# Two score computations placed between the second and third weight of an FFN step

## The chip, the cores and the metric

The kernel runs on one core of one Trainium2 chip. The metric is the device time of one execution in microseconds (us). A core has five engines that run their own instruction streams and meet only at semaphores: TensorE (PE, matrix products, with its weight loads shown as PEld), VectorE (DVE), ScalarE (ACT), GpSimd (POOL) and SyncE (SP). The last two mostly start transfers (DMAs) here. Products are written to PSUM, which has eight banks of 128 x 512 fp32; all other on-chip data are in SBUF.

## The reference

The computation is a low-rank attention (eight batches, eight heads, 1024 positions, head size 64; keys and values are projected from 1024 positions to 64), followed by a feed-forward network that takes the maximum of three products:

```python
k_proj = np.einsum('ks,bhsd->bhkd', E, k)
v_proj = np.einsum('ks,bhsd->bhkd', F, v)
scores = scale * np.matmul(q, k_proj.transpose(0, 1, 3, 2))
scores = scores - np.max(scores, axis=-1, keepdims=True)
attn = np.exp(scores)
attn = attn / (np.sum(attn, axis=-1, keepdims=True) + 1e-09)
attn_out = np.matmul(attn, v_proj)
x = attn_out.transpose(0, 2, 1, 3).reshape(8192, 512)
h = np.maximum(np.maximum(x @ w1, x @ w2), x @ w3)      # 512 -> 768
out = h @ w_out                                         # 768 -> 512
```

## The kernel before

The kernel goes through the eight batches. The feed-forward part of a batch is done in two halves (`ch` 0 and 1) of 512 positions. A half has six steps of `up` (`jt` 0 to 5, one for each 128 of the 768 hidden columns) and then four of `down` (128 positions each). In a step of `up`, PE makes twelve matmuls of 128 x 128 by 128 x 512: four for each of w1, w2 and w3, each weight into one PSUM bank. ScalarE copies the first bank to SBUF (`h1s`), VectorE takes the maximum of the copy and the second bank (`m12`) and then that of `m12` and the third bank (`hT`). `down` multiplies `hT` by w_out, ScalarE copies the result to `o_sb`, and SP's queue writes it out.

The attention of batch b+1 is laid between these steps while batch b's feed-forward part runs. `plan(b)` is a table from (half, step) to a list of pieces of attention; `behind(ch, step)` issues the pieces of an entry after that step. The pieces are:

- `qd`: VectorE repacks q, and SP's queue starts transposing transfers (line 331) that write q transposed into `qT`. For batch 1 there are two of them, one for each half of the head pairs, issued after step 7 of batch 0's first half.
- `kproj`, `kt`: the key projection (16 matmuls, L284), its transpose (L351) and a VectorE copy into `kpT`.
- `sc(b, g)`: scores of head pair g. Four small matmuls (L200, from `qT` and `kpT`) fill two banks. The exponential that reads them (`pT`, L211, ScalarE) isn't issued at once: it is put on the list `later`, which `run_later` works off in the next `up`, right after that step's `h1s` copy, or in the next `down` after its copy.
- `vproj`: the value projection (16 matmuls, L284) and four copies into `vp`, two on ScalarE and two on VectorE.
- `ld`: three loads for a batch further on, issued on POOL's queue.
- `za(b, g)`: the sums of the exponentials and the products with the values (L220, four matmuls each, two banks each), then on ScalarE the logarithm of the sums (`zl`, L233) and the exponential of its negative, the inverse (`zi`, L239), and on VectorE the product of the two (`xT`, L250), which frees the banks of the values.

The order of each engine's instructions is the order in which this code issues them. The PSUM banks are dealt by a small model of the engines' times inside the kernel (`clock`, `free`, `bank`, `two`): a new piece gets the bank, or the pair of banks, that the model expects to be free first. The semaphore waits follow from the data and from the banks dealt.

For the work around the change, batch 0's second half, the order before is: step 0, `kproj(1)`, step 1, `kt(1)`, step 2, then `sc(1,0)`, `sc(1,1)`, `vproj(1)`, `ld(2)`, step 3, `za(1,0)`, `sc(1,2)`, step 4, `za(1,1)`, `sc(1,3)`, step 5, `za(1,2)`, and the four `down` steps, with `za(1,3)` after the second of them.

Of the kernel before, what the change touches and what calls it, by code (L numbers as in the profile page):

```python
# [15 lines left out]
def kernel(  # L16
# [62 lines left out]
    def bank():  # L79
        n = min(range(8), key=lambda n: free[n])  # L80
        deal((n,))
        return psum_t[:, n, :], (n,)
# [5 lines left out]
    def runs(eng, ready, dt, ns=()):  # L88
        if eng in clock:
            clock[eng] = max(clock[eng], ready + 0.06) + dt  # L90
            for n in ns:
                free[n] = clock[eng]
            return clock[eng]
        return ready + dt
# [3 lines left out]
    def copy(eng, o, i, ns=(), dt=0.65):  # L98
        done = {  # L99
            "v": nc.vector.tensor_copy, "s": nc.scalar.copy, "g": nc.gpsimd.tensor_copy  # L100
        }[eng](out=o, in_=i)
        runs(eng, clock["pe"] if ns else 0.0, dt, ns)
        return done
# [89 lines left out]
    def scores(b, g, lo, nsi):  # L193
        t, ns = two()
        n = nsi // 2
        for c in range(2):
            for hp in range(2):
                rows = slice(hp * HALF, (hp + 1) * HALF)
                at = g * SI + lo + c * n
                nc.tensor.matmul(  # L200
                    out=t[c * HALF:(c + 1) * HALF, hp, 0:n * P],
                    lhsT=kpTs[b][rows, g, :],
                    rhs=qTs[b][rows, at:at + n, :],
                    start=True, stop=True,
                )
        return t[:, :, 0:n * P], ns, pe(n * MM / 4 + 0.1)

    def exps(b, g, lo, nsi, sc):
        t, ns, ready = sc
        pTs[b, g, lo] = att.tile([P, 2, CHUNK], BF16, name="pT", bufs=4)[:, :, 0:nsi * HALF]  # L210
        nc.scalar.activation(out=pTs[b, g, lo], in_=t, func=AF.Exp, scale=scale)  # L211
        runs("s", ready, 0.17 + nsi * 0.107, ns)
# [45 lines left out]
    def run_later():  # L258
        for f in later:
            f()  # L260
        later.clear()

    def sc(b, g, lo=0, nsi=SI):
        def f():
            t = scores(b, g, lo, nsi)
            later.append(lambda: exps(b, g, lo, nsi, t))
        return f
# [12 lines left out]
    def proj(b, kv, t, heads, width):  # L280

        for si in range(SI):
            for hh in range(2):
                nc.tensor.matmul(  # L284
                    out=t[hh * HALF:(hh + 1) * HALF, 0:width],
                    lhsT=efT[:, si, (kv - 1) * KP:kv * KP],
                    rhs=qkv[b][kv][:, heads[hh], si, :],
                    start=(si == 0), stop=(si == SI - 1),
                )
        pe(8 * (width * 0.00042 + 0.01))  # L290
# [72 lines left out]
    def vproj(b):  # L363
        def f():
            t, ns = bank()
            proj(b, 2, t, (LO, HI), 4 * D)

            vps[b] = att.tile([P, H, D], BF16, name="vp")
            for hh, hs in enumerate((LO, HI)):
                i = t[hh * HALF:(hh + 1) * HALF, 0:4 * D].rearrange("a (h d) -> a h d", d=D)  # L370
                for to in range(2):
                    copy("sv"[hh], vps[b][to * HALF:(to + 1) * HALF, hs, :], i, ns, 0.4)
        return f
# [120 lines left out]
    def up_mm(h, i, b, ch, jt, cts, first=0, last=NCT - 1):  # L494
        for ct in cts:
            nc.tensor.matmul(  # L496
                out=h,
                lhsT=w_sb[i][:, ct, jt * P:(jt + 1) * P],
                rhs=xTs[b][:, ct, ch * SPC:(ch + 1) * SPC, :],
                start=(ct == first),  # L500
                stop=(ct == last),
            )
            pe(MM)

    def most(o, h, ns, other, ready=0.0):
        nc.vector.tensor_tensor(out=o, in0=h, in1=other, op=ALU.max)  # L506
        return runs("v", max(clock["pe"], ready), 0.69, ns)
# [27 lines left out]
                most(hs[:, jt] if i == 1 else hTs[0, 0][:, jt, :], *h[jt], hs[:, jt])  # L535
                then((i, jt))

    def up(b, ch, jt):
        if jt == 0:
            hTs[b, ch] = ffn_sb.tile([P, NJT, CHUNK], BF16, name="hT")  # L540
        h, done = [], []
        early = jt == 0
        for i in range(3):
            h.append(bank())
            up_mm(h[i][0], i, b, ch, jt, range(NCT - early))
            done.append(clock["pe"])
        if early:
            for i in range(3):
                up_mm(h[i][0], i, b, ch, jt, (NCT - 1,))
                done[i] = clock["pe"]  # L550
        h1s = ffn_sb.tile([P, CHUNK], FP32, name="h1s")
        nc.scalar.copy(out=h1s, in_=h[0][0])  # L552
        r = runs("s", done[0], 0.6, h[0][1])
        run_later()
        m12 = ffn_sb.tile([P, CHUNK], FP32, name="m12")
        nc.vector.tensor_tensor(out=m12, in0=h[1][0], in1=h1s, op=ALU.max)  # L556
        runs("v", max(r, done[1]), 0.69, h[1][1])
        most(hTs[b, ch][:, jt, :], *h[2], m12)
# [50 lines left out]
    def ld(b):  # L609
        return lambda: load(b)  # L610

    def plan(b):
        n = b + 1
        if b == 0:
            c1 = (SPC, SPC)
            return {
                (0, 6): [za(0, 1, *c1), sc(0, 3, *c1)],
                (0, 7): [qd(1, 2), za(0, 2, *c1)],
                (0, 8): [za(0, 3, *c1)],
                (1, 0): [kproj(1)],  # L620
                (1, 1): [kt(1)],
                (1, 2): [sc(1, 0), sc(1, 1), vproj(1), ld(2)],
                (1, 3): [za(1, 0), sc(1, 2)],
                (1, 4): [za(1, 1), sc(1, 3)],
                (1, 5): [za(1, 2)],
                (1, 7): [za(1, 3)],
            }
        if b == 1:
            return {
                (0, 1): [qd(2)],  # L630
                (0, 5): [kproj(2), vproj(2), ld(3)],
                (0, 6): [kt(2)],
                (0, 7): [sc(2, 0)],
                (0, 9): [za(2, 0), sc(2, 1)],
                (1, 1): [za(2, 1), sc(2, 2)],
                (1, 3): [za(2, 2), sc(2, 3)],
                (1, 5): [za(2, 3)],
                (1, 6): [qd(3)],
            }
        if b == 2:  # L640
            return {
                (0, 2): [kproj(3), vproj(3), ld(4)],
                (0, 3): [kt(3)],
                (0, 4): [sc(3, 0)],
                (0, 6): [za(3, 0), sc(3, 1)],
                (1, 0): [za(3, 1), sc(3, 2), qd(4)],
                (1, 2): [za(3, 2), sc(3, 3), kproj(4), vproj(4), ld(5)],
                (1, 4): [kt(4)],
                (1, 5): [za(3, 3), sc(4, 0)],
            }  # L650
        if n == B:
            return {}
        out = {
            (0, 1): [za(n, 0), sc(n, 1)],
            (0, 3): [za(n, 1), sc(n, 2)],
            (0, 9): [za(n, 2), sc(n, 3)],
            (1, 3): [za(n, 3)],
        }
        if n + 1 < B:
            out[0, 6] = [qd(n + 1)]  # L660
            out[0, 9] += [kproj(n + 1), vproj(n + 1)]
            out[1, 1] = [kt(n + 1)]
            out[1, 3] += [sc(n + 1, 0)]
        if n + 2 < B:
            out[1, 1] += [ld(n + 2)]
        return out

    for b in range(B):
        p = plan(b)

        def behind(ch, step):
            for f in p.get((ch, step), []):
                f()

        for ch in range(NCHUNK):
            if (b, ch) == (0, 0):
                c1 = (SPC, SPC)
                up_first({
                    (0, 0, 5): [lambda: v_pair(2)],
                    (0, 1, 2): [lambda: x(2)],  # L680
                    (0, 1, 5): [lambda: v_pair(3), ld(1)],
                    (0, 2, 2): [lambda: x(3)],
                    (2, "a", 2): [qp(0, (0, 1), *c1)],
                    (2, "a", 4): [qp(0, (2, 3), *c1)],
                    (2, 0): [sc(0, 0, *c1)],
                    (2, 2): [sc(0, 1, *c1)],
                    (2, 4): [za(0, 0, *c1, then=True), sc(0, 2, *c1)],
                })
                run_later()
                behind(0, NJT - 1)  # L690
            else:
                for step in range(NJT):
                    up(b, ch, step)
                    behind(ch, step)
            for tt in range(SPC):
                down(b, ch, tt, "v" if (b, ch) == (0, 0) else "s")
                behind(ch, NJT + tt)
# [30 lines left out]
```

The softmax here doesn't subtract the row's maximum and nothing guards it: scores larger than these inputs give would overflow.

## Time and profile before

| | us |
|---|---|
| median of 7 runs | 406.52 |
| lowest and highest run | 405.8, 406.9 |
| the profiled execution's own time | 406.99 |
| its span, first to last instruction | 405.2 |
| PE busy in the span | 396.1 (98%) |
| DVE, ACT, POOL busy | 199.9, 190.9, 31.4 |
| granted PE clock, mean | 0.996 |

All times inside an execution are counted from the start of the span. The span leaves out 1.8 us that lie around the instructions, and the profiled execution took 0.47 us more than the median. A row of the lists gives start, length, engine, source line, operation, what is written and read, and the count of instructions merged into it; in brackets is the idle time ahead of it and what ended that. A row's matmuls overlap, since they are pipelined: twelve matmuls of 128 x 512, each recorded with about 380 ns, follow each other at 216 ns. The chain of work is followed back from the last instruction: at each step to what released it, or to the instruction ahead of it on its engine. Around 55 to 70 us it shows which engine set the pace at each moment.

### The profile page before, as it was taken

What the parts mean: (1) busy time and instruction counts of PE and PEld (TensorE: products, weight loads), DVE (VectorE), ACT (ScalarE), POOL (GpSimd) and SP (SyncE); (2) the same over time, 40 slices, a digit from 0 to 9 for tenths busy, and PEclk for the clock granted to TensorE, in tenths of its full rate; (3) what the DMA queues carried; (4) which work ended last, traced back from release to release, by engine and by line L of the source; (5) the groups of instructions that cost most, each with busy time, mean ns of one, the idle gap of its engine ahead of it and who ended that gap; (6) DMA issues with size and microseconds to landing.
All of it is one profiled execution on the core that took longest, in us unless ns stands there. A gap on an engine that the chain in (4) does not pass through costs nothing.

```text
span 405.2 us, 5913 instructions
## 1 busy us (share of the span) xinstructions
PE 396.1 (98%) x2374; PEld 178.6 (44%) x2374; DVE 199.9 (49%) x309; ACT 190.9 (47%) x278; POOL 31.4 (8%) x44
## 2 busy tenths in 40 slices
PE   7899999999999999999999999999999999999996
PEld 2444443444444545444544445444544444444443
DVE  2337856462655527527353655625464363525251
ACT  2611529624763366555544555437535556432322
POOL 7340011002000100200200002000000000000000
PEclk9989999999999999999999999999999999999999
DMA  8999999948927994991799119950510202020202
GB/s 142 206 206 207 219 216 172 239 110 124 255 37 207 170 247 105 142 243 32 211 180 182 53 31 238 205 150 2 138 72 1 104 2 104 2 104 0 105 0 104
DMA packets 62667, 53.33 MB, mean 132 GB/s; under 512 B 30128, under 2 KB 58288, under 8 KB 62640
## 3 DMA queue, kind: packets, MB, share of 16 engines
q0 software_dynamic: 28512, 28.31, 43.9%
q1 hardware_dynamic: 33984, 24.51, 19.5%
q8 instruction: 18, 0.29, 0.3%
q10 hardware_dynamic: 144, 0.13, 0.1%
q14 instruction: 9, 0.07, 0.1%
HBM read 57.15 MB, written 16.78 MB: 182 GB/s over the span
## 4 chain that ended last, share of the span: by engine, by line
PE 90%; DMA 4%; ACT 2%; DVE 1%; POOL 1%; issue 1%; DVEq 0%; ACTq 0%; POOLq 0%
PE banks L496 60%; PE banks L591 19%; PE banks L220 4%; DMA w_sb<-in_moe_w_dram 3%; PE banks L284 3%; PE banks L200 2%; DVE xT L250 1%; ACT pT L211 1%; ACT zl L233 1%; ACT zi L239 1%; DMA out_dram<-o_sb 0%; POOL k_t L147 0%; PE banks L425 0%; POOL q_t L152 0%; POOL v_t L147 0%
## 5 line engine op out<-in xcount | busy, mean ns | idle before, releaser
L496 PE MATMUL banks<-xT,w_sb 128*128 128x512 bf16 x1152 | 259.0, 381 | 1.2 <-DMA w_sb<-in_moe_w_dram 1.1
L496 PEld LDWEIGHTS <-w_sb 128*128 128x128 bf16 x1152 | 109.6, 98 | 138.2 <-issue 10.9
L556 DVE TENSOR_TENSOR m<-banks,h1s 128x512 f32<-128x512 f32 x90 | 62.0, 689 | 85.1 <-ACT h1s L552 53.8
L552 ACT COPY h1s<-banks 128x512 f32<-128x512 f32 x90 | 52.4, 582 | 89.9 <-PE banks L496 87.7
L591 PE MATMUL banks<-wout_sb,hT 128*128 128x512 bf16 x378 | 85.6, 380 | 0.1
L250 DVE TENSOR_TENSOR xT<-banks,zi 128x1024 bf16<-128x1024 f32 (+1 forms) x36 | 39.8, 1106 | 75.8 <-ACT zi L239 56.4
L506 DVE TENSOR_TENSOR hT<-banks,m 128x512 bf16<-128x512 f32 x90 | 62.3, 692 | 10.1 <-DVE m L556 0.5
L99 ACT COPY o_sb<-banks 128x512 f32<-128x512 f32 (+1 forms) x60 | 34.8, 580 | 53.0 <-PE banks L591 52.9
L591 PEld LDWEIGHTS <-hT 128*128 128x128 bf16 x378 | 35.9, 98 | 45.5 <-DVE hT L506 2.9
L233 ACT ACTIVATE zl<-banks 128x1024 f32<-128x1024 f32 (+1 forms) x36 | 33.5, 930 | 29.7 <-PE banks L220 28.9
L211 ACT ACTIVATE pT<-banks 128x1024 bf16<-128x1024 f32 (+1 forms) x36 | 33.2, 931 | 14.0 <-PE banks L200 14.0
L239 ACT ACTIVATE zi<-zl 128x1024 f32<-128x1024 f32 (+1 forms) x36 | 34.6, 962 | 1.1
L189 POOL DMA_DIRECT2D q_t<-in_q_dram x7 | 6.1, 878 | 203.8 <-DMA qT<-q_p 109.3
L284 PEld LDWEIGHTS <-efT 128*64 128x64 bf16 x256 | 12.8, 110 | 4.7 <-issue 4.2
L220 PE MATMUL banks<-pT,ones 64*64 64x512 bf16 (+1 forms) x144 | 13.9, 376 | 0.7 <-DVE xT L250 0.3
L200 PE MATMUL banks<-qT,kpT 64*64 64x512 bf16 (+1 forms) x144 | 13.7, 359 | 0.4 <-DVE m L556 0.3
L220 PE MATMUL banks<-pT,vp 64*64 64x512 bf16 (+1 forms) x144 | 13.3, 356 | 0.1
L99 DVE CAST vp<-banks 64x256 bf16<-64x256 f32 (+1 forms) x18 | 7.1, 396 | 9.7 <-PE banks L425 5.4
L220 PEld LDWEIGHTS <-ones 64*64 64x64 bf16 x144 | 4.5, 103 | 14.6 <-issue 13.5
L380 PE MATMUL banks<-warm 128*128 128x512 bf16 x24 | 8.8, 496 | 1.2 <-DVE warm L170 1.2
L99 DVE COPY q_p<-q_t 128x1024 bf16<-128x1024 bf16 x28 | 10.0, 419 | 0.0
L284 PE MATMUL banks<-k_t,efT 128*64 128x256 bf16 (+1 forms) x144 | 8.7, 263 | 1.0 <-DMA k_t<-in_k_dram 0.9
(46 smaller groups left out, 94.3 us busy)
## 6 DMA issues: line engine op xcount, KB each, us to landing
out_dram<-o_sb SPq DMA_DIRECT2D x30, 512.0 KB, 3.0
q_t<-in_q_dram POOLq DMA_DIRECT2D x7, 1024.0 KB, 9.6
k_t<-in_k_dram POOLq DMA_DIRECT2D x7, 1024.0 KB, 13.9
v_t<-in_v_dram POOLq DMA_DIRECT2D x7, 1024.0 KB, 19.8
w_sb<-in_moe_w_dram POOLq DMA_DIRECT2D x5, 384.0 KB, 12.7
k_t<-in_k_dram POOLq DMA_DIRECT2D x2, 512.0 KB, 9.4
v_t<-in_v_dram POOLq DMA_DIRECT2D x4, 256.0 KB, 12.8
wout_sb<-in_moe_w_out_dram POOLq DMA_DIRECT2D x1, 768.0 KB, 15.7
```

The costliest lines, as they stand in the source:

```text
L99: done = {"v": nc.vector.tensor_copy, "s": nc.scalar.copy, "g": nc.gpsimd.tensor_copy}[eng](out=o, in_=i)
L211: nc.scalar.activation(out=pTs[b, g, lo], in_=t, func=AF.Exp, scale=scale)
L220: nc.tensor.matmul(out=t[hp * HALF:(hp + 1) * HALF, c, 0:nsi * HALF], lhsT=w(rows, hp), rhs=p[rows, hp, :], start=True, stop=True,)
L233: nc.scalar.activation(out=zl, in_=t, func=AF.Ln)
L239: nc.scalar.activation(out=zi, in_=zl, func=AF.Exp, scale=-1.0)
L250: nc.vector.tensor_tensor(out=xTs[b][:, g, lo:lo + nsi, :].rearrange("a (c s) p -> a c (s p)", c=2), in0=t, in1=zi, op=ALU.mult,)
L284: nc.tensor.matmul(out=t[hh * HALF:(hh + 1) * HALF, 0:width], lhsT=efT[:, si, (kv - 1) * KP:kv * KP], rhs=qkv[b][kv][:, heads[hh], si, :], ...
L496: nc.tensor.matmul(out=h, lhsT=w_sb[i][:, ct, jt * P:(jt + 1) * P], rhs=xTs[b][:, ct, ch * SPC:(ch + 1) * SPC, :], start=(ct == first), st ...
L506: nc.vector.tensor_tensor(out=o, in0=h, in1=other, op=ALU.max)
L552: nc.scalar.copy(out=h1s, in_=h[0][0])
L556: nc.vector.tensor_tensor(out=m12, in0=h[1][0], in1=h1s, op=ALU.max)
L591: nc.tensor.matmul(out=o_ps, lhsT=hTs[b, ch][:, jt, tt * P:(tt + 1) * P], rhs=wout_sb[:, jt, :], start=(jt == 0), stop=(jt == NJT - 1),)
```

## The change

`up` takes a function `mid` and calls it after the matmuls of its second weight (`i == 1`), ahead of those of the third. Every step of `up` outside batch 0's first half is now given such a function, which issues the pieces under the key `(step, "mid")` of the plan. The plan has one such key, in batch 0's second half, step 2; `sc(1, 0)` and `sc(1, 1)` stand there now, and `vproj(1)` and `ld(2)` stay behind step 2. With their matmuls, their entries on the list `later` move as well, so that step 2's own `run_later` issues their exponentials.

```diff
-    def up(b, ch, jt):
+    def up(b, ch, jt, mid=None):
...
             h.append(bank())
             up_mm(h[i][0], i, b, ch, jt, range(NCT - early))
             done.append(clock["pe"])
+            if i == 1 and mid:
+                mid()
...
                 (1, 1): [kt(1)],
-                (1, 2): [sc(1, 0), sc(1, 1), vproj(1), ld(2)],
+                (1, (2, "mid")): [sc(1, 0), sc(1, 1)],
+                (1, 2): [vproj(1), ld(2)],
...
                 for step in range(NJT):
-                    up(b, ch, step)
+                    up(b, ch, step, lambda: behind(ch, (step, "mid")))
                     behind(ch, step)
```

## The prediction

> **What bounds the kernel now.** I read the engine shares first, then the chain of work that ended last around the place of the change, then ScalarE's and TensorE's instructions in order of time there, last the transfer that feeds the moved matmuls.
>
> From the page, busy time and chain:
>
> ```profile
> PE 396.1 (98%) x2374; PEld 178.6 (44%) x2374; DVE 199.9 (49%) x309; ACT 190.9 (47%) x278; POOL 31.4 (8%) x44
> PE 90%; DMA 4%; ACT 2%; DVE 1%; POOL 1%; issue 1%; DVEq 0%; ACTq 0%; POOLq 0%
> ```
>
> TensorE (PE) sets the time. No matmul is added or removed, so only what PE waits for can change. The chain in order of time (start, length, what) leaves PE at one place near the change:
>
> ```profile
> 55.17 2.59 PE banks L496 x12
> 57.76 0.56 PE banks L200 x8
> 58.32 0.99 PE banks L284 x16
> ...
> 60.32 0.59 ACT h1s L552
> 60.91 0.14 ACT pT L211
> 61.04 0.67 issue
> 61.72 1.03 ACT pT L211
> 62.75 0.93 ACT zl L233
> ...
> 63.70 1.06 ACT zi L239
> ...
> 64.78 1.24 DVE xT L250
> ```
>
> Here L200 x8 is the moved work, the two scores of batch 1; L284 x16 is the value projection; the x12 group is a whole FFN step. From 60.3 to 70 us the chain is a loop: sums (L220), logarithm `zl`, inverse `zi`, the scaling `xT` on VectorE, which frees the PSUM banks for the next sums. PE's own list shows the moved matmuls and the sums:
>
> ```profile
> 57.69 0.63 PE L200 MATMUL banks<-qT,kpT 64*64 64x512 bf16 x8
> 61.94 0.41 PE L220 MATMUL banks<-pT,ones 64*64 64x512 bf16 x4
> 66.06 0.41 PE L220 MATMUL banks<-pT,ones 64*64 64x512 bf16 x4 [0.17 <-DVE xT L250]
> 69.94 0.41 PE L220 MATMUL banks<-pT,ones 64*64 64x512 bf16 x4 [0.18 <-DVE xT L250]
> ```
>
> One round takes 69.94 - 66.06 = 3.88 us, and PE waits at the second and third sums (the brackets are only the part seen as idle). So a shift of the first `zi` reaches PE whole, whatever else PE does between. ScalarE's list shows what holds the first round:
>
> ```profile
> 60.80 1.95 ACT L211 ACTIVATE pT<-banks 128x1024 bf16<-128x1024 f32 x2
> 62.62 1.04 ACT L233 ACTIVATE zl<-banks 128x1024 f32<-128x1024 f32 x1
> 63.70 1.06 ACT L239 ACTIVATE zi<-zl 128x1024 f32<-128x1024 f32 x1
> ```
>
> The two exponentials keep ScalarE until 62.75, though the first sums are done at 61.94 + 0.41 = 62.35. Last, the instructions on qT, which the scores read, and kpT, the other operand:
>
> ```profile
> L331 SPq DMA_TRANSPOSE qT<-q_p x1: 6556/6556/6556, 46.8 to 46.8; - x1
> DMA to landing us min/median/max: 10.3/10.3/10.3
> L99 DVE COPY kpT<-banks x1: 280/280/280, 55.7 to 55.7; 128x256 bf16<-128x256 bf16 x1
> ```
>
> The transfer with the first half of qT starts at 46.82 (its row in the queue's list) and lands 10.3 us later, at 57.1; it has 0.5 us to spare before 57.69. kpT is ready at 56.0.
>
> **The direction.** The words given speak of eight more matmuls ahead of the scores. In the instruction lists of the two programs, the scores stood behind all twelve matmuls of FFN step 2 (batch 0, second half) and now stand behind eight: they move four matmuls up, and w3's four of that step move behind them. They were issued after the whole step, not ahead of it. I price that.
>
> **Part 1, when the scores can start.** The x12 group takes 2.59 us, 0.216 each, so four matmuls are 0.86 and PE is ready for the scores at 57.69 - 0.86 = 56.83. kpT (56.0) and the banks (last released at 55.8 and 56.0, by `hT` of step 1 and the kpT copy) are there. qT is not: 57.1, and a few hundredths from the landing to the first matmul. PE stands still for about 0.3 to 0.4; I take 0.35. This wait is new, and behind it stand w3's four matmuls, the value projection and all of step 3. Bounds from this row: 0 if the half lands 0.3 earlier, 0.86 if it lands so late that the old place waits too.
> [...]
>
> **Part 2, one more change of shape on PE.** Before: 128-row matmuls, scores (64x64 tiles), projection (128x64), 128-row matmuls. After: 128-row, scores, 128-row, projection, 128-row. In the chain, twelve L496 matmuls after a copy of L351's full-array transposes take 2.59 (55.17), after an L284 group 2.70 (52.37): a return to the full array costs 0.11. One more: +0.11. Bounds: 0, and 0.24 (between the scores and the next w1 group at 62.40 to 63.13, 0.73 for 0.24 of scores, there is also a bank wait, so half of the excess at most).
> [...]
>
> **Part 3, the first sums.** Nothing else between 57.69 and 61.94 makes PE wait (0.56 + 0.99 + 2.59 and 0.11 fill it). So the first sums start at 61.94 + 0.35 + 0.11 = 62.40. Their exponentials run right behind the copy of step 2's h1s instead of step 3's: scores at 57.2, two exponentials of 0.97 from 57.6, done at 59.6; the vp copies (0.74) follow the projection at about 59.8, h1s of step 3 at 60.8 to 61.4. ScalarE is then free when the sums end.
>
> **Part 4, from sums to the end.** Where ScalarE is free, `zi` starts 1.52 after the sums (66.06 to 67.58; 69.94 to 71.45 is 1.51). So the first `zi` starts at 62.40 + 1.52 = 63.92 instead of 63.70: **+0.22 us**. ScalarE's relief gives back 0.24 of the 0.46 that PE loses. The loop carries 0.22 to the second and third sums (66.28, 70.16). From there PE runs gapless; its next wait, at 98.51 for an o_sb copy, is on work that PE itself set going, so nothing absorbs the shift.
>
> **What costs nothing.** VectorE: `hT` of step 2 comes 0.9 later (58.8), inside the gap until its vp copies; the vp copies end at 61.5, and the values need them at 62.6. The scores' step issues no DMA. The three loads of batch 2 stay behind the projection; the value load waits for the projection's end (59.3, then 59.8), but POOL reaches it at 61.19, behind the q and k loads, the first of which waits for the second half of qT (issue 53.4, landing 58.9). SP's queue is untouched. PSUM: w3 of step 3 now takes a bank of the first exponential (read by 58.7, wanted at 61.4); other banks are only renumbered, and from the following down projection on every wait of the program is the same one. The second score pair of step 3 stops waiting at 62.4, which saves PE some 0.4, but the next sums wait for xT anyway.
>
> **Sum.** 405.2 of span becomes 405.4. The profiled execution took 406.99, so 1.8 lies around the span, and it stands 0.47 over the median of the runs, 406.52. The shift carries over: 406.52 + 0.2 = **406.7 us**, +0.05%. About 0.2% (0.8 us) is what a measurement of this kernel can tell from no change, so this is "same".
>
> **Rivals.**
> *A, the half of qT lands in time (faster).* The trace's landing came under a profile, with the transfer engines busy 90% or more in the page's slices there; an execution in which it lands by 56.8 has no new wait: sums at 62.05, `zi` at 63.57, -0.13 us: 406.4. That is the largest gain, since the first sums stay behind the same matmuls. It is not 0.2% either. Against it: 10.3 us is what the trace has, 0.3 too late.
> *B, it lands late (slower).* Place: the same wait. For each 0.1 us of landing after 57.1 the loss grows by 0.1, until 57.69, where the old order waits as well: 0.22 + 0.53 = +0.75: 407.3. If ScalarE's relief is worth nothing as well, it is 0.86 + 0.11 = +0.97: 407.5. It passes 0.2% only if the landing comes after 57.6 and the relief shrinks below 0.16. For it: 0.5 us of spare is 5% of a 10.3 us transfer. Against it: the scores show no wait at 57.69 now.
> *C, absorbed.* A later wait not set by PE takes the 0.22: 406.5. The nearest candidates are batch 2's loads: v issued at 61.2 lands 19.8 later, at 81, first read at 92. That doesn't hold PE, so C is weak.
>
> **How the numbers follow.** Forecast (loss of 0.1 to 0.6, landing near the trace's): 55%. A: 17%, C: 6%, B: 15%, something that I do not see, either sign: 7%. Cases of both signs are nearly all smaller than the bound. Over 0.2% slower: a third to a half of B, most of it with scatter on top, and most of the unseen, together with the forecast's upper end under scatter: 18%. Over 0.2% faster: A at its end with scatter, part of the unseen: 9%. Within: 73%. Range: A's -0.13 and B's +0.75, with about 0.5 below and 0.35 above for the scatter of a median (single runs reach 405.8 and 406.9): 405.9 to 407.6.
>
> **What would show it.** The scores' row at 57.2 with an idle time ended by the qT transfer or by nothing named; first sums near 62.4; both exponentials done before 60; `zl` following the sums without a queue; second and third sums near 66.3 and 70.2. Wrong if the scores start at 56.9 (A), after 57.7 (B), or if the rounds are not 3.88 any more.

## The result and the profile after

The changed kernel takes 408.38 us (median of 14 runs, 406.55 to 409.16); the kernel before, in all its runs by then, 406.48 (34 runs, 405.72 to 407.2). The ratio on record, an estimate from all runs and not the quotient of these two medians, is 1.004, with a 95% interval of 1.003 to 1.0049: slower by 0.4%, outside the range of the prediction (405.9 to 407.6), which had forecast no change.

The profiled execution of the changed kernel took 408.59, its span 406.8 (405.2 before). PE's busy time is about the same. What answers to the chain of before, from the chain of the changed kernel (start, length, what):

```profile
PE 395.8 (97%) x2374; PEld 178.5 (44%) x2374; DVE 200.1 (49%) x309; ACT 191.1 (47%) x278; POOL 31.6 (8%) x44
PE 87%; DMA 7%; ACT 2%; POOL 1%; DVE 1%; issue 1%; DVEq 0%; ACTq 0%; POOLq 0%
```

```profile
44.49 12.45 DMA qT<-q_p
56.94 0.04 issue
56.98 0.63 PE banks L200 x8
57.61 1.34 PE banks L496 x4
58.95 1.85 PE banks L284 x16
60.80 3.05 PE banks L496 x12
```

The transposing transfer is on the chain now: PE waits for it until 56.94. Behind it, w3's four matmuls take 1.34, the value projection 1.85 (0.99 before), the whole of step 3 3.05 (61.94 - 59.24 = 2.70 before). PE's own list of the changed kernel shows how long it stood still:

```profile
52.69 1.89 PE L496 MATMUL banks<-xT,w_sb 128*128 128x512 bf16 x8
56.98 0.63 PE L200 MATMUL banks<-qT,kpT 64*64 64x512 bf16 x8 [2.41 <-DMA qT<-q_p]
63.78 0.41 PE L220 MATMUL banks<-pT,ones 64*64 64x512 bf16 x4
67.67 0.41 PE L220 MATMUL banks<-pT,ones 64*64 64x512 bf16 x4 [0.35 <-DVE xT L250]
```

PE was through with the second weight at 54.6, not at 56.8 as in my sum, and waited 2.41 us. The first sums come at 63.78 (61.94 before), the second at 67.67 (66.06), and the 1.6 stays to the end of the span. Two things have to be explained: why PE was 2.3 us earlier than in the profile of before although all instructions up to there are the same, and why the matmuls behind the wait are slow. The windows view answers both. Its columns are the stretch, its length, the busy time of PE, PEld, DVE, ACT and POOL, then the granted clock of PE, the share of the transfer engines and GB/s. First the kernel before:

```profile
19.74:23.16 3.42, 3.42 (x15) 1.78 (x16) 0.00 (x0) 0.59 (x1) 2.22 (x3) 0.50 1.18 209
58.08:61.49 3.41, 3.41 (x35) 1.86 (x28) 1.50 (x4) 1.90 (x4) 2.03 (x3) 1.00 0.52 175
```

Then the changed kernel:

```profile
58.08:61.49 3.41, 3.41 (x21) 1.55 (x20) 0.69 (x1) 1.93 (x4) 2.14 (x3) 0.50 0.48 157
```

```profile
19.09:22.50 3.41, 3.41 (x24) 1.53 (x25) 0.91 (x2) 0.74 (x2) 2.21 (x3) 1.00 1.18 207
```

In the profiled execution of before, PE ran at half its clock from 19.74 to 23.16. That cost 1.7 us of its work, and w_sb had landed 0.65 later; so PE came to the scores 2.3 late, after the landing of qT. The execution of after had no such spell early, met the landing head on, waited, and had a spell of the same 3.41 us behind the wait, from 58.08 to 61.49. Six matmuls at the same early place show it in PE's lists, before and after:

```profile
19.68 2.72 PE L496 MATMUL banks<-xT,w_sb 128*128 128x512 bf16 x6 [1.13 <-DMA w_sb<-in_moe_w_dram]
```

```profile
19.03 1.47 PE L496 MATMUL banks<-xT,w_sb 128*128 128x512 bf16 x6 [1.03 <-DMA w_sb<-in_moe_w_dram]
```

The 14 runs of the changed kernel fall into two groups: five with a mean clock of 0.998 to 1.0, 406.55 to 407.1, and nine with 0.994 to 0.996, 408.25 to 409.16. Their medians are 407.06 and 408.69. One spell of 3.41 us at half the clock makes 1 - 1.7/406.8 = 0.996 of the mean.

My theory from here (W): the landing of qT's first half is set by the load on the transfer engines and comes at about 57 whatever PE does; without an early spell the old order waits for it as well, only less long, and with less work behind it; and the longer wait of the new order also halves the clock in most executions. The rivals: the dealt banks or the split itself cost the time (O); the wait is new and the early spell is the rule in the old program (M); the dips of the clock don't depend on the wait (K, C, D); the order of PE's queue doesn't matter, since the loop of the sums sets the time (Q); the landing follows the issue (I).

### The profile page after: what moved, and what is told of

Read it like the earlier page. It is cut to its first block, busy times and chain, and to the rows that moved or that the text cites. A ratio compares the mean times of both kernels' runs of the same rounds, so it can differ in the third digit from the quotient of the medians.

```text
span 406.8 us, 5916 instructions
## 1 busy us (share of the span) xinstructions
PE 395.8 (97%) x2374; PEld 178.5 (44%) x2374; DVE 200.1 (49%) x309; ACT 191.1 (47%) x278; POOL 31.6 (8%) x44
## 4 chain that ended last, share of the span: by engine, by line
PE 87%; DMA 7%; ACT 2%; POOL 1%; DVE 1%; issue 1%; DVEq 0%; ACTq 0%; POOLq 0%
PE banks L496 59%; PE banks L593 19%; PE banks L220 4%; PE banks L284 3%; DMA w_sb<-in_moe_w_dram 3%; DMA qT<-q_p 3%; PE banks L200 2%; DVE xT L250 1%; ACT zl L233 1%; ACT zi L239 1%; DMA out_dram<-o_sb 0%; POOL k_t L147 0%; ACT pT L211 0%; POOL q_t L152 0%; POOL v_t L147 0%
## 6 DMA issues: line engine op xcount, KB each, us to landing
w_sb<-in_moe_w_dram POOLq DMA_DIRECT2D x5, 384.0 KB, 12.5
v_t<-in_v_dram POOLq DMA_DIRECT2D x4, 256.0 KB, 12.2
```

## The experiments

All ran in three groups, each beside the kernel before on the same chip: its median was 406.10 (28 runs) in the first, 406.36 (27) in the second, 406.31 (11) in the third.

**The kernel before once more** (no edit).

> The kernel before, unchanged. Theory W (wait and clock): the first half of qT lands at a moment that the transfer queues set, about 57.0 us, whatever PE does (57.16 in the profile before, 56.95 after, though its issue lay 2.3 us apart). PE came to the scores 2.3 us later in the profile before only because its clock had been at one half for 3.4 us from 19.7 us on. So in executions without that early dip the old order waits for qT as well, from about 55.4 to 57.0, 1.6 us. Expected: median 406.5, single executions with mean clocks of both kinds, 0.996 and about 1.0, and in a profile without the early dip the scores start at 57.0 after a wait that the qT transfer ends. Rival M (mix): the early dip is what the old program always has and the wait is new with the change; then every execution has a clock near 0.996 and the scores start at 57.7 with no wait.

406.22 (12 runs; ratio 0.9998, 0.9988 to 1.0008). Ten of the 12 executions had a clock of 0.999 or 1.0. PE's list in this profile, which has no early spell:

```profile
53.65 2.75 PE L496 MATMUL banks<-xT,w_sb 128*128 128x512 bf16 x12
57.71 0.63 PE L200 MATMUL banks<-qT,kpT 64*64 64x512 bf16 x8 [1.30 <-DMA qT<-q_p]
61.95 0.41 PE L220 MATMUL banks<-pT,ones 64*64 64x512 bf16 x4
```

So the old order waits as well, 1.30 here, and its clock holds. M falls. The wait is less than the 1.6 expected, since w_sb was late in this execution (its first six matmuls start at 20.00, against 19.03 in the profile of the changed kernel), by more than the landing was (57.67, against 56.94). The first profile of before was a rare kind of execution (of the 40 runs of this kernel in the group, five have a clock of 0.995 or 0.996 and an ordinary time), and it owed the 0.5 us of spare that I read in it to its late PE. That its time (406.99) is that of this profile (407.04) is chance: both start the scores at 57.7, that one because PE came then, this one because the transfer landed at 57.67, the latest of all profiles. The other eleven executions took 405.7 to 406.66.

**The changed kernel without the transfer's landing.** The first two scores read batch 0's transposed q.

```diff
-                    rhs=qTs[b][rows, at:at + n, :],
+                    rhs=qTs[0 if b == 1 and g < 2 else b][rows, at:at + n, :],
```

> The changed kernel, but the first two scores of batch 1 read batch 0's transposed q instead of batch 1's, so that they do not need the transfer (the output of these heads is not the reference's; the count and size of all instructions are the same). Theory W: no wait of 2.4 us and no dip of the clock behind it (together some 2.4 + 1.7 us in the profile after): executions without an early dip end near 404.3, those with one near 406.3; median 404 to 406.3, clearly below both kernels. Rival O (the order itself): splitting the step, the dealt banks or ScalarE's order cost the 1.9 us; then the time stays near 408.4.

404.70 (7 runs; ratio 0.9958, 0.9943 to 0.9973), all at a clock of 0.999 or 1.0. O falls: the same split and the same banks, and 1.4 us faster than before.

**The wait filled.** Eleven matmuls on a constant tile ahead of the moved scores, in the place of the wait.

```diff
-                (1, (2, "mid")): [sc(1, 0), sc(1, 1)],
+                (1, (2, "mid")): [lambda: idle(11), sc(1, 0), sc(1, 1)],
```

> The changed kernel with eleven matmuls on a constant tile (128x512, 0.216 each, 2.4 us) ahead of the two moved scores, in the place where PE waits. They are added work. Theory W: PE comes to the scores at about 57.0 and waits for next to nothing, so the clock stays up there; the executions near 408.6 vanish and the times gather near 407.0 to 407.3, where the undisturbed-clock executions of the changed kernel are. An execution with an early dip would pay the fill, about 408.7. Rival K (the wait alone, the clock's dips being independent of it): the share of executions near 408.6 stays as it was, median 408.4. Rival O: 408.4 + 2.4 = 410.8.

407.06 (12 runs, 406.7 to 407.59; ratio 1.002, 1.001 to 1.003). No execution is near 408.6 and all 12 have a clock of 0.999 or 1.0, with 2.4 us more work on PE. The chain of this kernel shows the changed order at full clock:

```profile
57.34 0.04 issue
57.38 0.63 PE banks L200 x8
58.00 0.97 PE banks L496 x4
58.97 0.99 PE banks L284 x16
59.97 2.69 PE banks L496 x12
62.66 0.37 PE banks L220 x4
63.03 0.02 issue
63.05 1.03 ACT zl L233
64.09 0.02 issue
64.11 1.07 ACT zi L239
```

From the scores to the first sums it is 62.59 (PE's list) - 57.38 = 5.21, in the old order 61.95 - 57.71 = 4.24: 0.97 more behind the landing. From the sums to `zi` it is 1.52 against 63.71 - 61.95 = 1.76: 0.24 given back by ScalarE. Net 0.73.

**The scores one step later**, between the second and third weight of step 3.

```diff
-                (1, (2, "mid")): [sc(1, 0), sc(1, 1)],
+                (1, (3, "mid")): [sc(1, 0), sc(1, 1)],
```

> The scores between the second and third weight of the step after: step 3 instead of step 2, behind the value projection and eight matmuls. Theory W: PE comes to them 3.6 us later than in the changed kernel, at 58.2 without an early dip and at 60.5 with one, always after the landing, so no wait and no dip: executions without an early dip end near 404.5, those with one near 406.7; median clearly below 406.5 if the early dip is not the rule. Rival O: 408.4 or more, since the step is split all the same. My prediction's own mechanism (ScalarE held by late exponentials): 406.7 in all executions, as the exponentials come as late as before.

405.06 (10 runs, 404.61 to 405.7; ratio 0.9969, 0.9958 to 0.9981), all at a clock of 1.0: faster than both kernels, with the step split all the same. PE's list shows the scores without a wait:

```profile
56.44 1.90 PE L496 MATMUL banks<-xT,w_sb 128*128 128x512 bf16 x8
58.27 0.63 PE L200 MATMUL banks<-qT,kpT 64*64 64x512 bf16 x8
59.80 0.41 PE L220 MATMUL banks<-pT,ones 64*64 64x512 bf16 x4
```

It comes out above the 404.5 that was expected: `zl` started at 60.55 there, behind the late exponentials, as in the old order.

**The projection ahead of the scores**, at the old place, no step split.

```diff
-                (1, 2): [sc(1, 0), sc(1, 1), vproj(1), ld(2)],
+                (1, 2): [vproj(1), sc(1, 0), sc(1, 1), ld(2)],
```

> The kernel before with the value projection ahead of the two scores at the same place behind step 2, no split of a step. Theory W (the landing of qT at 56.7 to 57.7 is what PE waits for): PE comes to the scores one projection (0.99) later, at 56.4 instead of 55.4, so the wait falls from 1.3 (copy of the kernel before, scores at 57.71) to about 0.3 to 0.7; the projection itself may wait a little for v, which lands at 55.4 to 56.4. Gain of 0.6 to 1.0 on the kernel before: 405.1 to 405.5. Rival Q (queue order on PE does not matter, since the loop of sums, logarithm, inverse and scaling sets the time): no change, 406.1.

405.32 (12 runs; ratio 0.9981, 0.9973 to 0.999). In its profile the projection waits 0.70 for v and the scores then start at 56.97, right behind the landing (44.16 + 12.8 = 56.96) and with next to no wait. Q falls.

**The changed kernel once more** (no edit), on the second group's chip.

> The changed kernel, unchanged, beside the others on the same chip. Theory W: two groups of executions, some without a dip of the clock (0.998 to 1.0) about 0.7 to 0.9 over the kernel before, near 406.9, and some with one (0.994 to 0.996) about 1.6 higher, near 408.5. Rival C (the dips belong to the chip that ran first, and not to the wait): all executions near 406.9 with clock 0.999 or more, as with the filled wait.

407.95 (10 runs; ratio 1.0035, 1.0021 to 1.0048). Three executions at a clock of 1.0 took 406.92 to 407.18, five at 0.995 to 0.996 took 408.33 to 408.81. Two more, at 0.996, took 406.44 and 407.57; 406.44 would fit an execution with an early spell, 407.57 fits neither group, and their traces were not kept. C falls. The profiled execution, of 408.65, has the wait and slow scores behind it:

```profile
57.16 1.07 PE L200 MATMUL banks<-qT,kpT 64*64 64x512 bf16 x8 [2.58 <-DMA qT<-q_p]
```

**Half of the load of v left out**, and the projection reading heads 0 to 3 twice.

```diff
-            dma = nc.gpsimd.dma_start(out=tiles[i], in_=view((q, k, v)[i], b))
+            hs = slice(0, H // 2) if (i, b) == (2, 1) else slice(0, H)
+            dma = nc.gpsimd.dma_start(out=tiles[i][:, hs], in_=view((q, k, v)[i], b)[:, hs])
...
-            proj(b, 2, t, (LO, HI), 4 * D)
+            proj(b, 2, t, (LO, LO if b == 1 else HI), 4 * D)
```

> The changed kernel with half of the load of v for batch 1 left out: heads 0 to 3 alone are loaded, and the value projection reads them twice, so its output for heads 4 to 7 of that batch is not the reference's; no other instruction changes. 0.5 MB less at some 207 GB/s is 2.5 us of transfer time ahead of the landing of qT's first half. Theory W with the landing set by the load on the transfer engines: the landing moves from about 57 to about 54.5 to 55.5, PE's wait of 2.4 shrinks below 0.9, no dip, time 404.2 to 405.3. Rival I (the landing is set by the issue and by the transposing transfer's own 10 to 12 us): the landing stays within 0.4 of 57, time as the changed kernel's, 407 to 408.5.

404.92 (5 runs, 404.86 to 405.13; ratio 0.9969, 0.9957 to 0.9981), all at a clock of 1.0. The list of SyncE has the two transposes from 44.80 on, and the view of the tile qT the longer of their landings:

```profile
44.80 9.00 SPq L332 DMA_TRANSPOSE qT<-q_p  x2
```

```profile
DMA to landing us min/median/max: 4.6/6.9/9.3
```

The landing is at 44.80 + 9.3 = 54.1, 2.6 to 3.6 us earlier than in the other profiles, and the scores start at 54.82 with no wait. I falls. The issues and landings of all profiles say the same (each landing is the issue plus the time to landing in the view of qT):

| kernel | issue | to landing | landing |
|---|---|---|---|
| before, early spell | 46.82 | 10.3 | 57.1 |
| before with batch 0's q, early spell | 46.37 | 10.4 | 56.8 |
| before, copy | 45.46 | 12.2 | 57.7 |
| changed | 44.49 | 12.4 | 56.9 |
| changed, copy | 44.50 | 12.6 | 57.1 |
| changed with batch 0's q | 44.08 | 12.8 | 56.9 |
| changed, filled | 44.76 | 12.6 | 57.3 |
| projection first | 44.16 | 12.8 | 57.0 |
| one step later | 44.50 | 12.2 | 56.7 |
| behind the first weight of step 2 | 45.13 | 12.5 | 57.6 |
| behind the first weight of step 3 | 44.71 | 12.3 | 57.0 |
| changed, half of v | 44.80 | 9.3 | 54.1 |

With the full loads the issue moves by 2.7 us, the landing by 1.0 and not with it: the two earliest of these landings, 56.7 and 56.8, have an early and a late issue. What it does move with is the load of v ahead of it: with half of that it comes 2.6 us or more earlier. With full loads v lands at 26.51 + 29.1 = 55.6 in the profile of before and at 25.86 + 29.9 = 55.8 in that of the changed kernel (issue on POOL's queue plus the time to landing), and with the projection first PE's wait for v ends at 55.81; in these three the landing of qT comes 1.2 to 1.5 us later.

**The kernel before without the landing.** Batch 0's q again, in the old order (the edit of the second experiment).

> The kernel before, with the first two scores of batch 1 reading batch 0's transposed q (output of these heads not the reference's), the counterpart of the same edit on the changed kernel, which gave 404.70. Neither waits for the transfer, so their difference is what the move is worth apart from it: one more change of shape on PE (0.11) against ScalarE's earlier exponentials. My sum had the changed order 0.13 faster without the wait: 404.8 here. Rival O (the split of the step is a loss by itself): 404.3 or less here.

404.79 (12 runs; ratio 0.997, 0.9958 to 0.9982, against 0.9958, 0.9943 to 0.9973, of its counterpart). The intervals overlap, so the times can't tell 0.13 us. Two of the twelve executions, 406.58 (the profiled one; its clock is 1.00 from 55 to 66 us, and it comes to step 2 at 54.56, against 53.65 in the copy of before, so I take its spell for an early one) and 406.76, have a clock of 0.996 and take 1.8 to 2.0 us more than the median; with the landing in place, the old order's executions at 0.995 and 0.996 in the first group took 406.04 to 406.66, but for one of 408.1, against a median of 406.10. So the wait for qT hides most of an early spell, as it did in the profile of before; that this was an early spell in the runs without a kept trace is not shown. In the two profiles, from the first matmul of step 2 to `zi` it is 63.25 - 54.56 = 8.69 in the old order and 60.90 - 52.28 = 8.62 in the new one: 0.07 for the new.

**The scores four matmuls further ahead**, behind the first weight of step 2.

```diff
-            if i == 1 and mid:
+            if i == 0 and mid:
```

> The changed kernel with the two scores four matmuls further ahead: behind the first weight of step 2 instead of the second. Theory W: PE comes to the landing another 0.86 earlier and waits 3.2 to 3.5 instead of 2.4 to 2.6, and all that it did in that time follows later. Executions without a dip near 407.8 (0.86 over the changed kernel's 407.0), those with a dip near 409.4; if the dip hangs on the length of the wait, nearly all executions have one, where the changed kernel had 9 of 14 and about 6 of 10. Rival D (the share of dips does not depend on the wait's length): about 6 of 10 again.

409.58 (6 runs; ratio 1.0075, 1.0056 to 1.0095). One execution at a clock of 1.0 took 407.69; three at 0.994 to 0.996 took 409.41 to 409.70; two at 0.986 and 0.987 took 410.84 and 411.21. The last profile (0.987) has a wait of 3.37 us, and its windows view the clock at one half for two spells on end:

```profile
57.71 1.07 PE L200 MATMUL banks<-qT,kpT 64*64 64x512 bf16 x8 [3.37 <-DMA qT<-q_p]
```

```profile
55.00:57.70 2.70, 0.00 (x0) 0.00 (x0) 0.00 (x0) 0.00 (x0) 0.00 (x0) 0.76 1.28 175
57.70:60.20 2.50, 2.49 (x12) 0.77 (x12) 0.00 (x0) 1.80 (x2) 0.24 (x1) 0.50 1.08 337
60.20:62.70 2.50, 2.50 (x11) 0.85 (x11) 1.05 (x2) 0.14 (x1) 1.51 (x2) 0.50 0.45 27
62.70:66.00 3.30, 3.30 (x25) 1.82 (x22) 1.49 (x4) 1.31 (x3) 0.87 (x1) 0.92 1.12 171
```

A mean of 0.76 over 2.70 us is 1.3 us at one half, and 0.92 over 3.30 is 0.5; with the 5.0 between them that is 6.8 us, twice 3.41, from 56.4 on, while PE still stood. By my estimate this profile's mean clock of 0.987 is three spells of 0.4% each; where the third one lay is not shown. The other run's 0.986 is about as many, but its trace was not kept. Five of six executions dipped. Six runs are few against D; two spells on end were seen in no other profile.

**Behind the first weight of step 3.** Both edits together: `i == 0`, and the key `(1, (3, "mid"))`.

> The scores behind the first weight of step 3 (behind the value projection and four matmuls): four matmuls ahead of the place that gave 405.06. Theory W: PE comes to them at about 57.4 without an early dip, 0 to 0.4 after the landing, so next to no wait and no dip, and the exponentials end 0.86 earlier, so the logarithm of the first sums follows the sums directly: 0.2 to 0.4 better than the place behind the second weight, 404.7 to 405.0. If the landing comes later than 57.4 in many executions, the gain is lost: 405.1 to 405.4.

404.81 (5 runs; ratio 0.9963, 0.9951 to 0.9975). It can't be told from the place behind the second weight (0.9969, 0.9958 to 0.9981). In the profile `zl` follows the sums at once, but starts at 60.56, against 60.55 there: PE was at step 2 0.2 us later in this execution and began the projection 0.1 late, so the sums came at 60.10 instead of 59.80, which took back what the earlier exponentials gave.

## Why the prediction was wrong

**The direction** was read rightly: the scores had moved up, not back, and that is what made the wait.

**Part 1 is the step that failed.** It took 56.83 for PE's arrival and 57.1 for the landing from one execution and moved the scores against both as if the two belonged together. They don't. The arrival of that execution was 2.3 us late, by a spell of half clock and a late w_sb; the row of clocks in its profile had it in the third slice (an 8 among nines), in the lines of before that I did not show:

```profile
PEclk9989999999999999999999999999999999999999
```

The landing does not follow PE. So the wait was 2.41 and 2.58 in the two profiles of the changed kernel instead of 0.35, outside my bounds of 0 and 0.86, which had been drawn around that one arrival. Against the old order, which waits as well, the move adds the four matmuls' 0.86, my upper bound. The prediction took 10.3 us after the issue for the transfer's own length (rival B); it hung at least in part on the load of v: with half of that it was 9.3, against 12.4 in the changed kernel, at issues 0.3 apart.

**Parts 2 to 4 held.** With the wait filled, the new order has 0.97 more between landing and sums (0.86 + 0.11) and ScalarE gives back 0.24: the terms as they stood. Their sum, +0.73, is rival B's +0.75, for which I had asked for a late landing; in fact an early PE does the same and is the rule. The executions of the changed kernel at full clock have it: 407.06 against 406.48 (+0.6), and 407.09 against 406.36 (+0.7) in the copies. Rival A's -0.13 without the wait is 0.07 in the two profiles, too small for the times to confirm.

**What no part of the sum and no rival had is the second price of a wait.** By the wait alone the time would be 406.5 + 0.7 = 407.2, inside the range; it is the clock that takes it out. With PE standing for 2.41 and 2.58 us there came 3.4 us at half the clock in both profiles of the changed kernel (in the copy the windows show a clock of 0.85 from 55.00 to 57.70 and of 0.73 from there to 62.50, which is 0.8 and 2.6 us at one half, from about 56.9 on, just ahead of the scores). From the scores to the first sums it is 63.78 - 56.98 = 6.80 there, 5.21 at full clock: 1.6 us. By their times and clocks 14 of the 24 runs of the changed kernel paid it. Those lie 2.2 over the old order (medians 408.69 and 408.52, against 406.48 and 406.36), which is near 0.7 + 1.6; the rest of the runs pulls the medians of all down to 1.9 and 1.6 over it. That it is the standing still and not the place or the chip is shown by the fill (0 of 12), by the changed order without the landing (0 of 7), by the copy on another chip (5 of 10) and by the longer wait (5 of 6). What decides whether a given execution pays is not shown. The old order's 1.3 us mostly escapes it: one run of the 28 in the first group took 408.1 at 0.995, one of the 27 in the second 407.91 at 0.996.

**Rival C of the prediction** (absorbed later) was rightly called weak: the 1.6 us of the first sums reached the end of the span.

## What to carry to other kernels

Before a slack is read from one profile, look at the granted clock ahead of it, and ask which of the two sides follows PE: here PE's arrival shifted by 2.3 us with a late w_sb and a spell of half clock, while the landing of the transfer stayed within 1.0 us for issues 2.7 apart and came 2.6 us or more earlier with half the load of v. Work that needs a landing close by was better moved behind other ready work: of the 0.97 us that the change put behind the landing ScalarE gave back 0.24, and the scores one step later, or the projection ahead of them, gave 0.2 to 0.4% where four matmuls the other way cost some 0.2% at full clock. And the wait on TensorE was priced twice here: its own length, and, with waits of 2.41, 2.58 and 3.37 us in the profiles, half-clock spells of 3.4 us in part of the executions (14 of 24, and 5 of 6 with the longest wait).

## What the runs showed of the hardware

The spells of half clock lasted 3.41 us in the profiles of before (from 19.74 on) and of the changed kernel (from 58.08 on) and about 3.4 in its copy; with the wait of 3.37 us came 6.8 us at one half, two spells on end. In the profile of before the spell came after a wait of only 1.13 us at 19.7, at the end of a stretch in which PE was less busy (3.76 us of the 5 from 15 to 20); at the same place waits of 1.03 in the changed kernel (PE busy for 3.87 of the same 5 us) and of 1.29 in the copy of the kernel before left the clock alone, so the length of that wait does not decide it. And half a megabyte less in POOL's queue of loads brought the landing of a transfer on SP's queue forward by 2.6 us or more; 0.5 MB at the 207 GB/s that the transfer engines moved from 30 to 45 us in the profile of before would be 2.5, an estimate.
